# Sixteen dense matmuls ahead of the first scores of each full-attention loop

## The chip, the core and the metric

The program runs on one NeuronCore of one Trainium2 chip. The metric is the device time of one execution in microseconds (us), from the first to the last instruction. The profile's names for the engines are used: PE (TensorE, matmuls), PEld (its weight loads), DVE (VectorE), ACT (ScalarE), POOL (GpSimd).

## The reference, cut to what matters

Four residual blocks on x of shape (1, 2048, 512): local attention (A), full attention (B), A, B. Block B has 32 query heads of width 16 and one shared key/value head:

```python
def _B_ref(x, wq, wk, wv, wo):
    q = (x @ wq).reshape(B, S, H, Dh).transpose(0, 2, 1, 3)
    k = x @ wk
    v = x @ wv
    scores = einsum("bhqd,bkd->bhqk", q, k) * (Dh ** -0.5)
    p = softmax(scores, axis=-1)
    o = einsum("bhqk,bkd->bhqd", p, v)
    return o.transpose(0, 2, 1, 3).reshape(B, S, H * Dh) @ wo
```

## The kernel before

Block B is a prologue (layer norm, projections, and a flag that says whether exp may run without a maximum), then a loop over 2048 chunks of 128 keys x 512 queries of one head. Three chunks make a tile, so there are 683 tiles in a loop, and two loops.

```python
    def emit_scores(i):                       # PE: K = 32 rows per matmul, three of four row groups
        st = stp.tile([128, tile_chunks, 512], F32, name="st")
        for n, (qc, t, a, kt, g) in enumerate(cs):
            nc.tensor.matmul(st[:, n, :], lhsT=KAB[32 * g:32 * g + 32, a, ...],
                             rhs=QT[32 * g:32 * g + 32, t, ...], ..., tile_position=(32 * g, 0))

    def emit_exp(i):                          # ACT: one exp over 3 PSUM banks
        nc.scalar.activation(out=pt[...], in_=st_tiles[i][...], func=AF.Exp, scale=scale)

    def emit_outproj(n, now=None):            # PE: y, 128x128x512, four per block of 64 chunks
        ...
            y = ypp.tile([128, D], F32, name="y")
            nc.tensor.matmul(y[:], lhsT=onb[:, cols], rhs=wo_pad[:, t, a, :], start=True, stop=True)
            nc.vector.tensor_tensor(out=x_sb[:, qt, :], in0=x_sb[:, qt, :], in1=y[:], op=ALU.add)

    def emit_pv(i):                           # PE: all 128 rows, three of four groups of 32 columns
            nc.tensor.matmul(o_ps[(qc, t, a)][32 * g:32 * g + 32, :], lhsT=VE[:, kt, :],
                             rhs=pt[:, n, :], ..., tile_position=(0, 32 * g))

    for i in range(min(st_bufs, ntiles)):     # st_bufs = 2
        emit_scores(i)
    for i in range(ntiles):
        emit_exp(i)
        if i + st_bufs < ntiles:
            emit_scores(i + st_bufs)
        emit_pv(i)
        if i % op_every == op_every - 1:      # op_every = 3
            emit_outproj(1, now=i)
```

A scheduler then decides the order of the instructions on each engine; the program's order is only its starting point. PSUM, an on-chip memory, holds two st tiles of three chunks each, and one buffer each for o_ps and y.

## Time and profile before

| | before |
|---|---|
| device time, median of the first 3 runs | 2389.79 us (2388.62 to 2390.17) |
| attention loops, first exp to last exp | 955.2 and 956.3 us: 80% of the span |
| ACT busy in the loops | 97% |
| granted PE clock in the loops | 0.50 |
| an ordinary tile / a tile with a y | 1.34 us / 1.62 us |

From the page of the kernel before, the busy share in 40 equal slices of the span (9 is 90% or more), and the granted PE clock in tenths of full speed:

```profile
PE   5887899999999999999877879999999989999996
ACT  5314999999999999999842169999999999999996
PEclk9998555555555555555589975555555555555555
```

The clock is full for most of the local-attention blocks and half in both loops. In numbers, from the windows view (stretch in us, its length, then busy us and instruction count of PE, PEld, DVE, ACT and POOL, then clock, DMA share, GB/s). The first two lines are the two clock windows around the start of the first loop, the others lie inside the loops:

```profile
224.84:228.25 3.41, 1.02 (x4) 0.28 (x3) 2.33 (x5) 0.00 (x0) 0.00 (x0) 1.00 0.00 0
228.25:231.66 3.41, 1.06 (x6) 0.23 (x7) 0.33 (x3) 0.67 (x1) 0.38 (x1) 0.50 0.00 0
500.00:700.00 200.00, 181.94 (x886) 43.52 (x883) 57.48 (x63) 194.59 (x144) 0.00 (x0) 0.50 0.00 1
1600.00:1800.00 200.00, 182.10 (x886) 43.57 (x886) 53.27 (x60) 194.59 (x143) 0.00 (x0) 0.50 0.01 3
```

PE waits for the flag just before the loop, and the clock falls there. Inside, ACT is 97% busy and PE 91%.

The groups of instructions that carry the loop (count, then busy us and mean ns of one, then the engine's idle time before them and what ended most of it):

```profile
L511 ACT ACTIVATE pt<-st 128x1536 bf16<-128x1536 f32 (+1 forms) x1366 | 1860.7, 1508 | 63.9 <-PE st L503 62.0
L503 PE MATMUL st<-QT,KAB 32*128 32x512 bf16 x4096 | 859.4, 597 | 176.1 <-ACT pt L511 168.2
L520 PE MATMUL y<-wo_pad,onb 128*128 128x512 bf16 x256 | 155.3, 607 | 20.6 <-DVE onb L537 12.3
```

And the timeline of a stretch in which ordinary tiles turn into tiles with a y (start, duration, what, count, and in brackets the idle time just before and what ended it; lines of PEld and DVE are left out):

```profile
265.47 0.61 PE L503 MATMUL st<-QT,KAB 32*128 32x512 bf16 x3
...
266.81 0.61 PE L503 MATMUL st<-QT,KAB 32*128 32x512 bf16 x3 [0.18 <-ACT pt L511]
267.35 0.61 PE L547 MATMUL o_ps<-pt,VE 128*32 128x512 bf16 x3
267.90 0.61 PE L520 MATMUL y<-wo_pad,onb 128*128 128x512 bf16 x1
268.44 0.61 PE L503 MATMUL st<-QT,KAB 32*128 32x512 bf16 x3
...
269.52 0.61 PE L520 MATMUL y<-wo_pad,onb 128*128 128x512 bf16 x1
270.06 0.61 PE L503 MATMUL st<-QT,KAB 32*128 32x512 bf16 x3
...
272.41 1.45 ACT L511 ACTIVATE pt<-st 128x1536 bf16<-128x1536 f32 x1 [0.18 <-PE st L503]
```

Read the distance between the starts of two st groups. From 265.47 to 266.81 it is 1.34 us, and PE waits 0.18 us for ACT: ACT sets the pace. From 266.81 to 268.44, with a y, it is 1.63 us, without a wait on PE: PE sets the pace, and at 272.41 ACT waits for PE. Notice too that the y stand in consecutive tiles although the program emits one every three tiles. That is the scheduler's doing.

### The profile page before, as it was taken

How to read it: one execution, taken by the hardware profiler on the slowest of the kernel's cores; microseconds unless marked ns; L12 is line 12 of the kernel's file. 1: busy time of each engine (PE TensorE's matmuls, PEld its weight loads, DVE VectorE, ACT ScalarE, POOL GpSimd, SP SyncE). 2: the span in 40 equal slices, each digit the busy share in tenths (PEclk: the TensorE clock that was granted, in tenths of full speed). 3: DMA queues.
4: the chain of work that ended last, by engine and by line, in shares of the span. 5: the costliest groups of instructions: out<-in, count | busy, mean ns of one | idle time of the engine just before them, and what ended most of it. 6: DMA issues, size and time to landing. Idle time of an engine off the chain costs nothing.

```text
span 2389.7 us, 27720 instructions
## 1 busy us (share of the span) xinstructions
PE 2085.2 (87%) x11652; PEld 611.5 (26%) x11652; DVE 839.2 (35%) x1061; ACT 2015.7 (84%) x1603; POOL 35.7 (1%) x67
## 2 busy tenths in 40 slices
PE   5887899999999999999877879999999989999996
PEld 5433222222222222222153332222222222222221
DVE  3875222232223222322339832222222222222222
ACT  5314999999999999999842169999999999999996
POOL 1002000000000000000010000000000000000000
PEclk9998555555555555555589975555555555555555
DMA  1101000000000000000000000000000000000000
GB/s 63 37 2 28 1 1 1 1 1 1 1 1 1 1 1 1 1 1 1 1 3 2 1 1 1 1 1 9 1 1 1 1 10 1 1 9 1 1 1 11
DMA packets 14315, 11.56 MB, mean 5 GB/s; under 512 B 7904, under 2 KB 13536, under 8 KB 14048
## 3 DMA queue, kind: packets, MB, share of 16 engines
q1 hardware_dynamic: 13120, 8.60, 1.4%
q8 instruction: 95, 1.56, 0.3%
q10 hardware_dynamic: 1056, 1.05, 0.1%
q14 instruction: 44, 0.36, 0.1%
HBM read 7.37 MB, written 2.10 MB: 4 GB/s over the span
## 4 chain that ended last, share of the span: by engine, by line
ACT 39%; PE 31%; issue 17%; DVE 12%; POOL 0%; DMA 0%; ACTq 0%; SPq 0%; DVEq 0%; POOLq 0%
ACT pt L511 38%; PE st L503 11%; PE o_ps L547 8%; PE y L520 6%; DVE lb L536 3%; PE ps L184 3%; DVE prod L209 2%; PE y L265 1%; PE ps L359 1%; DVE pv L253 1%; PE acc L256 1%; DVE ot L528 1%; DVE lb L535 1%; DVE onb L537 1%; DVE qsq L373 0%
## 5 line engine op out<-in xcount | busy, mean ns | idle before, releaser
L511 ACT ACTIVATE pt<-st 128x1536 bf16<-128x1536 f32 (+1 forms) x1366 | 1860.7, 1508 | 63.9 <-PE st L503 62.0
L503 PE MATMUL st<-QT,KAB 32*128 32x512 bf16 x4096 | 859.4, 597 | 176.1 <-ACT pt L511 168.2
L547 PE MATMUL o_ps<-pt,VE 128*32 128x512 bf16 x4096 | 864.7, 607 | 1.4 <-ACT pt L511 1.0
L528 DVE COPY ot<-o_ps 128x512 f32<-128x512 f32 x64 | 44.3, 692 | 1163.2 <-PE o_ps L547 1163.2
L503 PEld LDWEIGHTS <-KAB 32*128 32x128 bf16 x4096 | 236.5, 99 | 766.1 <-issue 764.0
L547 PEld LDWEIGHTS <-VE 128*32 128x32 bf16 x4096 | 154.4, 101 | 621.4 <-issue 621.3
L521 DVE TENSOR_TENSOR x_sb<-x_sb,y 128x512 f32<-128x512 f32 x256 | 176.1, 688 | 226.1 <-PE y L520 226.1
L536 DVE RECIPROCAL lb<-lb 128x512 f32<-128x512 f32 (+1 forms) x70 | 214.9, 3075 | 2.1
L520 PE MATMUL y<-wo_pad,onb 128*128 128x512 bf16 x256 | 155.3, 607 | 20.6 <-DVE onb L537 12.3
L89 ACT ACTIVATE xn<-x_sb,ln_nmr,ln_rstd 128x512 bf16<-128x512 f32 x44 | 33.3, 806 | 92.0 <-DVE ln_nmr L83 88.8
L209 DVE TENSOR_TENSOR prod<-Qch,Kch 128x4096 bf16<-128x4096 bf16 x32 | 72.4, 2279 | 58.1 <-ACT Kch L188 56.7
L184 PE MATMUL ps<-xnT,w_sb 128*32 128x512 bf16 x1536 | 90.7, 392 | 1.9 <-ACT Vch L188 1.9
L184 PEld LDWEIGHTS <-w_sb 128*32 128x32 bf16 x1536 | 80.1, 141 | 12.1 <-issue 7.5
L256 PE MATMUL acc<-pv,ident 128*128 128x512 bf16 x256 | 68.7, 402 | 15.9 <-DVE pv L253 10.3
L212 PE MATMUL lg<-prod,ident 128*128 128x512 bf16 x256 | 60.6, 379 | 18.8 <-DVE prod L209 18.8
L258 ACT CAST Och<-acc 128x2048 bf16<-128x2048 f32 x8 | 14.9, 1866 | 72.2 <-PE acc L256 72.2
L253 DVE TENSOR_TENSOR pv<-attn,Vch 128x2048 bf16<-128x2048 bf16 x64 | 73.2, 1222 | 1.5 <-PE acc L256 1.5
L214 ACT ACTIVATE L<-lg 128x512 f32<-128x512 f32 x16 | 9.6, 598 | 70.7 <-PE lg L212 70.7
L99 PE MATMUL pT<-ident,xn 128*128 128x128 bf16 x256 | 27.6, 256 | 44.6 <-ACT xn L89 29.8
L520 PEld LDWEIGHTS <-onb 128*128 128x128 bf16 x256 | 26.4, 103 | 131.6 <-issue 89.7
L535 DVE STREAM_SHUFFLE lb<-ot 128x512 f32<-128x512 f32 (+1 forms) x70 | 46.8, 673 | 0.0
L537 DVE TENSOR_TENSOR onb<-ot,lb 128x512 bf16<-128x512 f32 (+1 forms) x70 | 44.6, 641 | 2.1
(89 smaller groups left out, 538.8 us busy)
## 6 DMA issues: line engine op xcount, KB each, us to landing
xi<-in_A_x_dram SPq DMA_DIRECT2D x4, 512.0 KB, 5.6
wo_r_73<-in_A_wo_dram SPq DMA_DIRECT2D x4, 512.0 KB, 8.2
w_sb<-in_A_wqkv_dram SPq DMA_DIRECT2D x4, 384.0 KB, 8.2
out_dram<-xo SPq DMA_DIRECT2D x2, 512.0 KB, 3.0
out_dram<-xo ACTq DMA_DIRECT2D x2, 512.0 KB, 4.9
wq_sb<-in_B_wq_dram SPq DMA_DIRECT2D x4, 128.0 KB, 3.2
woB_sb<-in_B_wo_dram SPq DMA_DIRECT2D x4, 128.0 KB, 3.7
wo_pad<-in_B_wo_dram SPq DMA_DIRECT2D x16, 32.0 KB, 1.8
```

Source lines behind the costliest of these rows:

```text
L184: nc.tensor.matmul(ps[32 * c:32 * c + 32, :], lhsT=wqkvP[:, kt, j, d, :], rhs=xnT[:, kt, c * 512:(c + 1) * 512], start=(kt == 0), stop=(kt ...
L209: nc.vector.tensor_tensor(out=prod[:], in0=Q[:, dsl, :], in1=K[:, dsl, PAD - DIL * w:PAD - DIL * w + 512], op=ALU.mult)
L253: nc.vector.tensor_tensor(out=pv[:], in0=attn[:, w, :].unsqueeze(1).to_broadcast([PCH, DG, 512]), in1=V[:, ds_, PAD - DIL * w:PAD - DIL * ...
L256: nc.tensor.matmul(acc[:, i, :], lhsT=ident[:PCH, :PCH], rhs=pv[:, i, :], start=(w == 0), stop=(w == W - 1))
L503: nc.tensor.matmul(st[:, n, :], lhsT=KAB[32 * g:32 * g + 32, a, kt * 128:(kt + 1) * 128], rhs=QT[32 * g:32 * g + 32, t, qc * 512:(qc + 1) ...
L511: nc.scalar.activation(out=pt[:, :len(cs), :], in_=st_tiles[i][:, :len(cs), :], func=AF.Exp, scale=scale)
L520: nc.tensor.matmul(y[:], lhsT=onb[:, cols], rhs=wo_pad[:, t, a, :], start=True, stop=True)
L521: nc.vector.tensor_tensor(out=x_sb[:, qt, :], in0=x_sb[:, qt, :], in1=y[:], op=ALU.add)
L535: nc.vector.stream_shuffle(out=lb[:, sl], in_=ot[:, sl], mask=[16] * 32)
L536: nc.vector.reciprocal(out=lb[:, sl], in_=lb[:, sl])
L537: nc.vector.tensor_tensor(out=onb[:, sl], in0=ot[:, sl], in1=lb[:, sl], op=ALU.mult)
L547: nc.tensor.matmul(o_ps[(qc, t, a)][32 * g:32 * g + 32, :], lhsT=VE[:, kt, :], rhs=pt[:, n, :], start=(kt == 0), stop=(kt == NT - 1), tile ...
```

## The change

The intent: PE is at half clock for the whole loop. A burst of dense matmuls raises the clock, so put one ahead of the first scores, so that the loop starts at full clock.

```diff
@@ attn_B_fast
+    warm = ypp.tile([128, D], F32, name="y")
+    pe_filler(nc, warm[:], wo_pad[:, 0, 0, 0:128], wo_pad[:, 0, 0, :], 16)
     for i in range(min(st_bufs, ntiles)):
         emit_scores(i)
```

`pe_filler` issues 16 matmuls of 128x128x512 into a tile that nobody reads. In PE's instruction order they stand after the branch on the flag and before the first scores; nothing else moves on any engine.

## The prediction

> **What bounds the kernel now.** The windows view gives each attention loop about 960 us (230-1190 and 1414-2375 us): 80% of the span. There ACT is 97% busy, PE 91%, granted clock 0.50 throughout. The timeline shows the two regimes. An ordinary tile takes 1.342 us and is set by ACT (eleven exps fill 14.88 us with no idle; PE waits 0.18 us per tile for ACT). A tile that also carries an output projection (y) takes 1.62 us and is set by PE: st, o_ps and y start 0.54 us apart. The groups list puts the whole price of the half clock at 62 us: ACT's idle time before the exps released by st. That, 2.6%, is the ceiling of what a full clock could give here.
>
> **What the change adds.** Sixteen 128x128x512 matmuls after the flag branch and before the first scores, twice, with nothing to overlap: the first exp needs the scores, which stand behind them on PE. Nothing is removed or reordered (I compared the instruction order). The existing filler at the end of the local-attention layer is the same shape: 16 per 3.41 us at full clock, 213 ns each; such dense matmuls took 427 ns at half clock. At half clock the burst lasts 6.8 us, at full 3.4.
>
> **The clock.** The Trainium skill, "TensorE: Matmul & The Clock Gate", Part 1, says the array is throttled by default, is released after a busy window of about 3.4 us and throttled again after an idle one. This trace's clock records agree on the length (every state lasts a multiple of 3.413 us) but not that only an idle window throttles. I counted streamed columns per window:
> - Released: windows with an array share near 1 (dense matmuls, four-way tiled matmuls), lowest 0.8.
> - Never released in 960 us: attention at half clock, 0.64 to 0.79 of the window streaming but only 3 of 4 row or column groups filled.
> - Throttled from full: windows streaming 0.25, 0.32, 0.33, 0.38 and 0.44. Kept for long: 0.5 and more.
>
> Just before each loop the clock falls (228 and 1412 us), since PE idles while the flag is computed. So the burst starts cold, runs cold for 3.4 to 6.8 us depending on where it meets the window grid, and finishes at full clock: 5.1 to 6.8 us, about 5.9. Then attention at full clock would stream 2 x 0.213 us per 1.342 us tile: 0.32 of a window, three quarters of the array. That is in the range that got throttled, so I expect the clock back at 0.50 within one or two windows (3.4-7 us), and it doesn't come back. In those windows no y exists, ACT sets the pace, so the full clock saves only about 0.3 us on the first scores.
>
> **Sum.** 2 x (5.9 - 0.3) = +11 us on the critical path, all of it: 2401 us, +0.5%. Range 2396 to 2405. Faster by over 2%: 0.05; within 2%: 0.93; slower: 0.02.
>
> **Right or wrong in the profile.** (1) A new group of 32 filler matmuls, about 12 us in all, with ACT idle about 12 us longer before the exps. (2) Clock 1.00 for one or two 3.41 us windows around the burst's end, then 0.50 for the rest of the loop. (3) Ordinary tiles still 1.342 us, y tiles 1.62 us, idle before exps by st otherwise about 62 us.
>
> **What would make it wrong.** If the loop holds the full clock once it has it (the throttle criterion could count time occupied, not columns), y tiles fall to ACT's 1.35 us and up to 62 us return: about 2340 us, just at the 2% line. If it holds for part of the loop, the result lies between. If the grid favours the burst, +9 us; if it never releases, +13.

## The result

The changed kernel took 2401.27 us (median of 4, 2392.05 to 2403.36) beside 2389.98 us of the kernel before: ratio 1.0045, interval 1.0023 to 1.0068. It is slower by about 11 us, clear of noise.

The clock row of the page of the changed kernel, and its groups:

```profile
PEclk9999555555555555555579985555555555555555
L511 ACT ACTIVATE pt<-st 128x1536 bf16<-128x1536 f32 (+1 forms) x1366 | 1860.5, 1513 | 75.3 <-PE st L503 73.2
L503 PE MATMUL st<-QT,KAB 32*128 32x512 bf16 x4096 | 857.4, 596 | 207.3 <-ACT pt L511 189.3
```

And the burst, from the list of groups that keeps shapes apart (30 of its 32 matmuls were recorded):

```profile
L111 PE MATMUL y<-wo_pad 128*128 128x512 bf16 x30 | 10.9, 527 | 5.4 <-DVE flags L399 5.1 <-issue 0.2
```

ACT's busy time is the same. Its idle time before the exps rose from 63.9 to 75.3 us, by 11.4 us, and the burst was busy for 10.9 us: these are the 11 us. The timeline of the first loop's head shows it happen. In the kernel before (PEld and other lines left out, here and below):

```profile
230.15 1.06 PE L503 MATMUL st<-QT,KAB 32*128 32x512 bf16 x6 [2.77 <-DVE flags L399]
230.99 14.88 ACT L511 ACTIVATE pt<-st 128x1536 bf16<-128x1536 f32 x11 [6.62 <-PE st L503]
```

and in the changed kernel:

```profile
229.79 4.43 PE L111 MATMUL y<-wo_pad 128*128 128x512 bf16 x10 [2.71 <-DVE flags L399]
234.44 1.56 PE L111 MATMUL y<-wo_pad 128*128 128x512 bf16 x5 [0.22 <-issue]
235.93 0.60 PE L503 MATMUL st<-QT,KAB 32*128 32x512 bf16 x6
236.53 26.97 ACT L511 ACTIVATE pt<-st 128x1536 bf16<-128x1536 f32 x20 [12.45 <-PE st L503]
...
239.37 0.39 PE L503 MATMUL st<-QT,KAB 32*128 32x512 bf16 x3 [0.62 <-ACT pt L511]
...
243.40 0.61 PE L503 MATMUL st<-QT,KAB 32*128 32x512 bf16 x3 [0.19 <-ACT pt L511]
```

The scores start at 235.93, 6.14 us after the burst does, and ACT waits 12.45 us for them instead of 6.62. At 239.37 a group of scores takes 0.39 us instead of 0.61, but PE only waits longer for ACT (0.62 instead of 0.18 us); ACT goes on without a gap. At 243.40 everything is as before. The clock windows around it, from the windows view cut at the clock's own steps, and a stretch of the loop:

```profile
228.25:231.66 3.41, 1.87 (x5) 0.74 (x6) 0.28 (x2) 0.00 (x0) 0.27 (x1) 0.50 0.03 5
231.66:235.08 3.42, 3.20 (x8) 1.22 (x8) 0.00 (x0) 0.00 (x0) 0.00 (x0) 0.50 0.00 0
235.08:238.49 3.41, 1.92 (x16) 0.50 (x14) 0.00 (x0) 1.96 (x2) 0.00 (x0) 1.00 0.00 0
238.49:241.90 3.41, 1.70 (x15) 0.66 (x13) 0.00 (x0) 3.41 (x4) 0.00 (x0) 1.00 0.00 0
241.90:245.32 3.42, 2.89 (x18) 0.75 (x17) 0.00 (x0) 3.42 (x4) 0.00 (x0) 0.50 0.00 0
500.00:700.00 200.00, 178.28 (x879) 43.45 (x883) 57.52 (x63) 194.50 (x144) 0.00 (x0) 0.50 0.00 1
```

Full clock for two windows, 235.1 to 241.9 us, then half for the rest of the loop.

Where the time lies, worked out from each trace as the first exp's start to the last exp's end of each loop, and the stretches around them (us). All experiments are in it, so that it need not be repeated:

```
kernel                     span   up to loop 1  loop 1  between  loop 2   tail
before                   2389.7       231.0      955.2    228.6    956.3   18.6
the change               2399.4       236.5      955.5    233.7    956.2   17.5
e1 burst of 32           2407.2       239.1      955.3    239.0    956.2   17.4
e2 burst on 32 rows      2401.2       236.7      955.3    235.4    956.3   17.5
e10 burst on 32 columns  2401.8       236.9      955.3    235.7    956.4   17.5
e7 burst in prologue     2385.0       228.0      955.5    227.7    956.2   17.7
e8 the change again      2389.7       231.8      955.2    229.0    956.2   17.5
e3 two per tile          2346.9       235.9      927.0    236.6    929.0   18.4
e5 one per tile          2333.7       233.0      922.4    234.0    926.8   17.5
e6 two, 32 columns       2344.9       233.6      927.6    236.3    929.9   17.4
e9 two, 32 rows          3298.4       233.6     1408.0    231.0   1407.0   18.8
e4 y spread out          2334.8       226.8      930.9    228.3    931.3   17.5
e11 e4 + e5 + e7         2327.1       228.0      932.0    227.4    922.6   17.2
e12 e4 + e5              2341.0       227.6      932.2    230.3    933.6   17.3
```

The change left both loops at 955 and 956 us. It lengthened the stretch before each by 5 us. 683 tiles at 1.331 us, the distance of exps that follow each other without a wait, would take 909 us, so each loop holds 46 us more than that. Counted from the starts of the exps, 17 us of it stand around the 32 copies of o_ps that end the blocks, and 29 us elsewhere, nearly all in tiles with a y.

### The profile page after: what moved, and what is told of

It reads as the page before. It is cut to its first block, busy times and chain, and to the rows that moved or that the text cites. A ratio compares the mean times of both kernels' runs of the same rounds, so it can differ in the third digit from the quotient of the medians. Undisturbed runs are those within 1.5% of the kernel's fastest.

```text
span 2399.4 us, 27700 instructions
## 1 busy us (share of the span) xinstructions
PE 2061.3 (86%) x11602; PEld 614.8 (26%) x11684; DVE 839.1 (35%) x1061; ACT 2015.3 (84%) x1603; POOL 35.6 (1%) x67
## 4 chain that ended last, share of the span: by engine, by line
ACT 37%; PE 33%; issue 17%; DVE 12%; POOL 1%; DMA 0%; SPq 0%; ACTq 0%; DVEq 0%; POOLq 0%
ACT pt L511 36%; PE st L503 11%; PE o_ps L547 10%; PE y L520 4%; DVE lb L536 3%; PE ps L184 3%; DVE prod L209 2%; PE y L265 1%; PE ps L359 1%; DVE pv L253 1%; PE acc L256 1%; DVE lb L535 1%; DVE ot L528 1%; DVE onb L537 1%; DVE ln_stats L79 0%
## 5 line engine op out<-in xcount | busy, mean ns | idle before, releaser
L511 ACT ACTIVATE pt<-st 128x1536 bf16<-128x1536 f32 (+1 forms) x1366 | 1860.5, 1513 | 75.3 <-PE st L503 73.2
L520 PE MATMUL y<-wo_pad,onb 128*128 128x512 bf16 x198 | 120.1, 606 | 16.4 <-DVE x_sb L521 15.8
```

The source lines that it names most:

```text
L511: nc.scalar.activation(out=pt[:, :len(cs), :], in_=st_tiles[i][:, :len(cs), :], func=AF.Exp, scale=scale)
```

## The experiments

The theory from the prediction: the burst costs its own duration, because ACT has nothing to do until the scores come; it does raise the clock, but attention at full clock uses too little of PE to keep it. The rivals: the burst is too small; the burst does harm in itself; the clock is worth nothing to this loop; what costs time in the loop is not the clock but the order. Further runs asked what it is about the work that raises and keeps the clock.

### e1: 32 instead of 16

```diff
-    pe_filler(nc, warm[:], wo_pad[:, 0, 0, 0:128], wo_pad[:, 0, 0, :], 16)
+    pe_filler(nc, warm[:], wo_pad[:, 0, 0, 0:128], wo_pad[:, 0, 0, :], 32)
```

> Theory (the burst pays only for itself; attention at full clock streams about 0.32 of a window and is throttled again): 16 more matmuls per loop run at full clock, 0.213 us each, so 3.4 us more per loop than with 16: about 2408 us (2404 to 2412). The clock stays at 1.00 during the longer burst and falls back to 0.50 at most two windows (6.9 us) after its end. Rival (a bigger run-up holds the clock for the loop): the clock stays at 1.00 long into the loop and the time falls below that of the kernel before, by up to 50 us.

Measured: 2405.54 us (ratio to before 1.0068, interval 1.0046 to 1.0091). The bursts lasted 9.45 and 9.77 us. The clock stood at 1.00 from 234.1 to 244.3 us, three windows of which the burst itself filled the first, and then at 0.50. A longer run-up buys nothing: the rival is out.

### e2 and e10: a burst on a quarter of the array, by rows and by columns

```diff
-    pe_filler(nc, warm[:], wo_pad[:, 0, 0, 0:128], wo_pad[:, 0, 0, :], 16)
+    for _ in range(16):                      # e2: 32 rows, 128 columns
+        nc.tensor.matmul(warm[:], lhsT=wo_pad[0:32, 0, 0, 0:128], rhs=wo_pad[0:32, 0, 0, :],
+                         start=True, stop=True, tile_position=(0, 0))
+    for _ in range(16):                      # e10 instead: 128 rows, 32 columns
+        nc.tensor.matmul(warm[0:32, :], lhsT=wo_pad[:, 0, 0, 0:32], rhs=wo_pad[:, 0, 0, :],
+                         start=True, stop=True, tile_position=(0, 0))
```

> Sixteen matmuls of the same length but on 32 of the 128 rows: the same streaming time, a quarter of the array. Theory (the throttle weighs how much of the array is filled): the clock is never released, the burst takes 16 x 0.427 = 6.8 us per loop, no window of the loop shows 1.00, time about 2404 us. Rival (the throttle counts only the time in which the array streams): released as with the dense burst, two windows at 1.00, about 2401 us.

> The head burst on 128 rows and 32 columns: a quarter of the array again, like the burst on 32 rows that didn't release the clock, but with all rows in use. If release weighs the filled share of the array: not released, no window of the loop at 1.00, about 2403 us. If it weighs the rows in use: released as with the dense burst, two windows at 1.00.

Measured: e2 2402.43 us (ratio 1.0058, interval 1.0035 to 1.0081), e10 2403.52 us (one run). The windows of e2, from the burst's second window on:

```profile
230.60:234.00 3.40, 3.40 (x9) 1.17 (x8) 0.00 (x0) 0.00 (x0) 0.00 (x0) 0.50 0.02 5
234.00:237.40 3.40, 2.94 (x11) 0.73 (x10) 0.00 (x0) 0.67 (x1) 0.00 (x0) 0.50 0.00 0
```

and of e10:

```profile
231.90:235.30 3.40, 3.40 (x9) 1.17 (x8) 0.00 (x0) 0.00 (x0) 0.00 (x0) 0.50 0.00 0
235.30:238.70 3.40, 1.91 (x17) 0.52 (x15) 0.00 (x0) 1.84 (x2) 0.00 (x0) 1.00 0.00 0
```

The two full windows (230.60 and 231.90) look alike: PE busy all the time, one matmul after another every 0.427 us, a quarter of the array filled. On 32 rows the clock stays at half, on 128 rows it rises. Both loops of each run agree. So neither the time in which PE is busy nor the share of the array decides; the rows in use do, or something that goes with them, such as the rows of data that are read: no run here tells these apart. The e2 burst lasted 16 x 0.427 = 6.8 us, of which 0.85 us ran beside scores on the other row groups.

### e7: the burst where PE idles anyway

The prologue has a switch for such a filler. Nothing is added at the loop's head.

```diff
-def layer_B(..., flag_slot=None, fillB=0,
+def layer_B(..., flag_slot=None, fillB=16,
```

> No burst at the loop's head; 16 dense matmuls in the prologue instead, in PE's idle time while the flag is computed (8 before the last n2 matmuls, where PE idles 1.9 us, 8 behind them, where it idles 2.7 us; 8 take 1.7 us at full clock). Theory: the burst's cost is its place on the path to the first scores, so here it costs nothing (within 1 us per loop); the loop starts at 1.00 and falls to 0.50 within two windows (up to 7 us), loops of 955.5 us as before; time within 2 us of the kernel before, 2387 to 2391 us. Rival (the dense burst itself slows the loop, for instance by a clock limit): about 2401 us again.

Measured: 2387.89 us over 6 runs (ratio 0.9998, interval 0.9983 to 1.0013), loops 955.5 and 956.2 us. The same sixteen matmuls cost nothing here. What the change costs is its place. They also gained nothing: in this run the clock fell at 229.5 us, 1.5 us after the first exp of the loop, and no y comes that early.

### e3 and e5: dense matmuls in every tile, to keep the clock

If the clock falls because attention at full clock uses PE too little, more work must keep it. The extra matmuls write into the st tile and are overwritten by the scores behind them.

```diff
         st_tiles[i] = st
+        for f in range(2):                   # e5: range(1)
+            nc.tensor.matmul(st[:, f, :], lhsT=wo_pad[:, 0, 0, 0:128], rhs=wo_pad[:, 0, 0, :],
+                             start=True, stop=True)
```

The head burst of the change stays in.

> The head burst as in the change, and two dense matmuls before the scores of every tile to hold the clock. At full clock the array share would be 0.24 + 2 x 0.213/1.342 = 0.56 of a window, streaming 0.64: windows like that kept the clock in the kernel before. Theory: the clock stays at 1.00 through both loops; y tiles fall from 1.62 us to ACT's 1.34 us; ACT's idle before the exps falls from 62 us to about 25; time about 2345 us (2335 to 2360). Caution: the scheduler also spreads the y matmuls over three tiles each in this build, so part of the gain may be the order. Rival 1 (attention can't hold the clock whatever is added): 0.50 and PE-bound tiles of about 2 us, so 2800 us or more. Rival 2 (the half clock costs nothing, ACT sets the pace everywhere): clock 1.00 but no gain, about 2401 us.

> The head burst as in the change and one dense matmul before the scores of every tile. In this build the four y of a block still stand in four tiles running, as in the kernel before, so a gain here is the clock's alone. At full clock the array share would be 0.24 + 0.213/1.342 = 0.40 of a window, streaming 0.48; the kernel before dropped a window of 0.44 and kept windows of 0.50, so it is open whether the clock holds. If it holds: a y tile needs about 1.3 us of PE, less than ACT's 1.34, so each loop takes about 930 us instead of 955.5 and the time is about 2350 us (2340 to 2360). If it doesn't: 3 x 0.54 = 1.6 us of PE per tile at half clock, 683 x 0.28 = 190 us more per loop, about 2750 us. If the gain of the two-matmul version was only the order of the y: clock 1.00, loops of 955 us, 2401 us.

Measured: e3 2342.6 us (ratio 0.9805, interval 0.9787 to 0.9823), e5 2338.42 us (0.9799, 0.9780 to 0.9818), a little below its range. The window of 0.44 that e5's expectation speaks of is a misreading, for which see the end. The clock held, in e3 from 233.8 to 1165.7 us. The stretch from 500 to 700 us, first of e3, then of e5:

```profile
500.00:700.00 200.00, 190.01 (x1211) 58.10 (x1211) 55.61 (x60) 198.78 (x149) 0.00 (x0) 1.00 0.00 1
```

```profile
500.00:700.00 200.00, 161.07 (x1063) 44.63 (x1066) 55.52 (x62) 199.28 (x149) 0.00 (x0) 1.00 0.00 1
```

ACT is above 99% busy, at clock 1.00. In e5 the y still stand in consecutive tiles, as before, so its gain is the clock's alone. From its timeline:

```profile
270.61 0.39 PE L523 MATMUL y<-wo_pad,onb 128*128 128x512 bf16 x1
271.00 0.38 PE L503 MATMUL st<-wo_pad 128*128 128x512 bf16 x1
271.30 0.39 PE L506 MATMUL st<-QT,KAB 32*128 32x512 bf16 x3
...
271.95 0.39 PE L523 MATMUL y<-wo_pad,onb 128*128 128x512 bf16 x1
```

A tile with a y now takes 271.95 - 270.61 = 1.34 us, ACT's pace, although it carries one more matmul. So the clock is worth 956 - 925 = 31 us per loop (loops of 922.4 and 926.8 us), 62 us in all, and the rival that it is worth nothing is out. In e5 the margin is thin: the clock fell once, at 1879 us, and came back 13.7 us later.

### e4: the order of the y, without any filler

In e3, but not in e5, the scheduler had spread the y out by itself. That called for a run of the order alone, at half clock and without a burst:

```diff
-            nc.tensor.matmul(y[:], lhsT=onb[:, cols], rhs=wo_pad[:, t, a, :], start=True, stop=True)
+            last_y[0] = nc.tensor.matmul(y[:], lhsT=onb[:, cols], rhs=wo_pad[:, t, a, :], ...)
+            order_after(tc, last_y[0], last_pv[0])     # behind the o_ps matmul emitted last
```

> No burst and no filler: the kernel before with each y matmul tied behind the o_ps of the tile at which the program emits it, so that the four y of a block stand three tiles apart in PE's order instead of in four tiles running. Rival to 'the half clock costs 62 us': the bunching costs it. An ordinary tile leaves PE 0.26 us free (1.342 less 2 x 0.54), and three tiles with one y need 3 x 1.08 + 0.54 = 3.78 us of PE against 3 x 1.342 = 4.03 us of ACT, so ACT should hardly wait: if the bunching is the cause, about 45 to 60 us less, 2330 to 2345 us, with the clock still 0.50. If the half clock itself is the cause, no change.

Measured: 2338.46 us (ratio 0.9793, interval 0.9771 to 0.9815), loops 930.9 and 931.3 us. From its timeline:

```profile
269.04 0.61 PE L522 MATMUL y<-wo_pad,onb 128*128 128x512 bf16 x1
269.58 0.61 PE L505 MATMUL st<-QT,KAB 32*128 32x512 bf16 x3
...
270.67 0.61 PE L505 MATMUL st<-QT,KAB 32*128 32x512 bf16 x3
...
271.98 0.61 PE L505 MATMUL st<-QT,KAB 32*128 32x512 bf16 x3 [0.16 <-ACT pt L513]
...
273.07 0.61 PE L522 MATMUL y<-wo_pad,onb 128*128 128x512 bf16 x1
```

After each y PE catches up: the next two tiles take 1.09 and 1.31 us, and at 271.98 PE waits for ACT again before the next y. The group of exps in this kernel shows what is left:

```profile
L513 ACT ACTIVATE pt<-st 128x1536 bf16<-128x1536 f32 (+1 forms) x1366 | 1839.2, 1588 | 36.0 <-PE st L505 35.8
```

Most of what the full clock can give, 25 of 31 us per loop, is to be had at half clock by order alone. The clock was at 0.50 throughout the loops. Counted as above, the first loop of e4 keeps 18 us around the copies of o_ps and 4 us elsewhere, that of e5 12 us and 1 us. So order and clock both remove the stall of the y; what the clock removes besides is a part of the wait at the changes of block.

### e6 and e9: keeping the clock with narrow matmuls

Two per tile as in e3, but on a quarter of the array: e6 on 128 rows and 32 columns, e9 on 32 rows and 128 columns. e9 uses the row group of the first score, in that score's bank.

```diff
         st_tiles[i] = st
+        for f in range(2):                   # e6
+            nc.tensor.matmul(st[0:32, f, :], lhsT=wo_pad[:, 0, 0, 0:32], rhs=wo_pad[:, 0, 0, :],
+                             start=True, stop=True, tile_position=(0, 0))
+        for f in range(2):                   # e9 instead
+            gq = cs[0][4]
+            nc.tensor.matmul(st[:, 0, :], lhsT=wo_pad[32 * gq:32 * gq + 32, 0, 0, 0:128],
+                             rhs=wo_pad[32 * gq:32 * gq + 32, 0, 0, :], start=True, stop=True,
+                             tile_position=(32 * gq, 0))
```

> As the kernel with the head burst and two matmuls per tile, but the two use 32 of the 128 columns of the array: the same streaming time (0.64 of a window at full clock), array share only 0.24 + 0.08 = 0.32. If staying at full clock depends on the filled share of the array: throttled within two or three windows of the burst, PE-bound tiles of 4 x 0.5 = 2 us, 2 x 683 x 0.6 = 800 us more, about 3200 us. If it depends on the time in which the array streams: 1.00 through both loops and about 2345 us.

> As the run with two narrow matmuls per tile, but narrow in rows (32 of 128) instead of columns (32 of 128). That run kept the clock at an array share of 0.32, so the filled share of the array is not what keeps it; it may be the rows in use or the streaming time. At full clock: streaming about 0.63 of a window in both; share of rows in use 0.60 there, 0.36 here. If streaming time keeps the clock: 1.00 through both loops, about 2345 us. If the rows in use do: throttled within three windows, PE-bound tiles of about 1.8 us, 2950 us or more.

Measured, one run each: e6 2346.85 us, e9 3300.33 us. The stretch from 500 to 700 us, e6 and then e9:

```profile
500.00:700.00 200.00, 188.39 (x1197) 47.86 (x1203) 54.03 (x61) 198.76 (x148) 0.00 (x0) 1.00 0.00 1
```

```profile
500.00:700.00 200.00, 198.11 (x793) 39.08 (x794) 40.86 (x48) 140.18 (x98) 0.00 (x0) 0.50 0.00 1
```

With all rows in use the clock holds, although only a third of the array is filled on average. With 32 rows it fell within two windows and never came back in the loop, and PE then paced the loop at 2.06 us per tile (1408/683), more than the 1.8 us expected. It is the rows again: the windows before the two falls streamed for 0.48 and 0.60 of their time with a row use of 0.37 and 0.34, those of e6 inside its loops, streaming for 0.52 to 0.76, had a row use of 0.47 and more.

### What the clock follows, over all traces

For every clock window of 3.413 us in the fourteen traces I worked out three shares from the matmul records (start, shape, columns streamed at the granted clock): the time in which any matmul streams, the same weighted with the part of the array filled, and the same weighted with the rows in use out of 128 (matmuls on different row groups at the same time add up). The windows before a trace's first clock record count as half clock: the matmuls there start 0.427 us apart. Then I looked for the one threshold per share that best tells the windows after which the clock changed:

```
                          4159 windows at full clock       some 5800 at half clock   
                          121 of them followed by half     121 of them followed by full
weighted by               best threshold, misplaced        best threshold, misplaced
rows in use               0.355,   7                       0.745,   4
array filled              0.205,  52                       0.745,   8
time streaming only       0.36,   13                       0.895,  38
```

Rows do best on both sides; most windows are clear-cut by any of the three, so it is the pairs e2/e10 and e6/e9 that carry the argument. With rows, the overlap at full clock lies between 0.36 and 0.39. Some matmul records are missing from traces, which makes a share too low, and this settles three of the four misplaced at half clock (0.63 to 0.66 before a rise in the loops of e5, e11 and e12). Each of these windows lacks one y matmul, whose weight load and whose add on DVE are recorded. With it they reach 0.75 to 0.78. When all missing y of the loops are put back in all traces in this way, rows misplace one window at half clock, the filled array 8 and the time 38. The one left (e8 at 1209.3 us, 0.69, transposes only) lacks no record that I can see and stays open. So, on this core: below a row use of about 0.37 in a window the full clock falls, and from about 0.75 the half clock rises. This describes the traces that it was fitted on; it is not a statement of how the hardware is built.

It explains the loop. At full clock an ordinary tile streams its scores for about 0.216 us on three row groups and its o_ps for 0.216 us on all rows: (0.75 + 1) x 0.216 / 1.34 = 0.28 of the window, below 0.37, so it falls. One dense matmul more adds 0.16: 0.44, and holds, with little to spare. At half clock the busiest windows of the kernel before reach 0.74, just too little to rise by themselves.

### e8: the change again

> The change again, for the spread of its times: one of its four runs took 2392 us and the others 2401 to 2403. Theory: the burst costs 3.4 to 6.8 us per loop depending on where it meets the free-running windows, so runs between +6 and +13 us, 2395 to 2403, centre 2400; a run at 2392 should be rare and be as low as the lowest runs of the kernel before at that moment. Loops of 955.5 us in the profile, clock at 1.00 for two windows of each.

Measured: 2398.1 us (6 runs, 2391.45 to 2403.26), ratio 1.0043, interval 1.0025 to 1.0061. The profiled run was one of the two low ones, 2391.45 and 2391.8 us; so runs as low as this are not rare, which I had expected them to be. Its loops were 955.2 and 956.2 us and its bursts 5.50 and 5.73 us, 11.2 us in all, as before. It was short in the stretches before the loops (231.8 and 229.0 us against 236.5 and 233.7). Its clock record has fewer windows at half clock in the local-attention blocks: between 127 and 185 us it never falls, where the first profile of the change fell at 163 us, and before the third block's projections it rises at 1213 us, not at 1228. So the low runs are a matter of where the clock windows meet the rest of the program; the grid of the windows is not tied to it (the first clock record lies between 33.9 and 37.3 us in the fourteen traces). The other traces agree. Without prologue filler, PE's first instruction behind the flag of loop 1 starts at 225.7 to 226.7 us in the six traces whose clock holds for 58 us from about 127 us on (e4, e5, e6, e8, e9, e12), and at 228.9 to 230.3 us in the six whose clock also falls near 163 us. That accounts for the low profile; that it accounts for each single time is likely and not shown. The kernel before shows a similar spread (2382.01 to 2391.25 us in these rounds).

### e11 and e12: put together

e11 is e4's order, e5's one matmul per tile and e7's filler in the prologue, without the burst at the head. e12 is e11 without the prologue filler.

> What the runs point to, put together: the y three tiles apart, one dense matmul per tile to keep the clock, and the 16 dense matmuls in the prologue's idle time instead of at the loop's head. Loops of 920 to 927 us instead of 955.7, and no burst on the path: 2 x 32 us less than the kernel before, about 2325 us (2316 to 2334); clock 1.00 nearly all the way. If the clock adds nothing to the spread order, loops of 931 us and about 2338 us.

> The same without the 16 matmuls in the prologue: is any run-up needed? The loop starts at 0.50 with tiles bound by PE at about 1.6 us, streaming 0.80 of a window. If such windows release the clock (in the run with one matmul per tile it fell once in mid-loop and came back after 13.7 us), it comes within about 15 us, for a loss of some 3 us per loop: about 2331 us. If they don't, 2 x 683 x 0.27 us more: about 2700 us.

Measured over 5 runs each: e11 2334.94 us (ratio 0.9777, interval 0.9754 to 0.9801), just above its range, e12 2344.47 us (0.9811, 0.9797 to 0.9826). The second loop of e11 ran at full clock from its start and took 922.6 us, as expected. In its first loop the clock fell at 229.2 us and rose only at 280.4, so that loop took 932.0. In e12 the clock rose 54 and 59 us after the start of the loops, not within 15 us as I had expected: at half clock those windows use 0.73 to 0.74 of the rows, a hair below the threshold. What carried them over it was a y. The first y of a loop comes some 51 us after its start, in e12 here (the matmul's own record is missing, but not its weight load and its add):

```profile
278.35 0.61 PE L553 MATMUL o_ps<-pt,VE 128*32 128x512 bf16 x3
278.89 0.10 PEld L525 LDWEIGHTS <-onb 128*128 128x128 bf16 x1 [0.44 <-issue]
279.30 0.63 PE L505 MATMUL st<-wo_pad 128*128 128x512 bf16 x1 [0.33 <-issue]
279.54 0.69 DVE L527 TENSOR_TENSOR x_sb<-x_sb,y 128x512 f32<-128x512 f32 x1 [8.99 <-PE st L508]
```

The clock rose at 281.3 us, at the end of that window; in e11 too at the end of the window with the first y, in e12's second loop of that with the second (row use 0.747, recorded in full). So a run-up is not needed, but it saves some 9 us where it works. e11 has the lowest ratio, 2.2% below the kernel before; against e4 alone (ratio 0.9793, in other rounds) the intervals overlap, as with e3 and e5, so that the clock adds to the order is shown for loop 2 of the trace, but not for the whole time.

## Why the prediction was right

- **The time.** 2401 us was predicted, 2401.27 measured; six more runs gave 2398.1. The range 2396 to 2405 held the medians. It did not hold every run: 2391 and 2392 occurred. That the first median came within 0.3 us is luck, as single runs spread over 12 us; what the runs support is some 10 us (ratios 1.0045 and 1.0043).
- **The burst is on the critical path.** Right. Its first matmul to the first score took 6.14 and 4.86 us, 11.0 in all, against 2 x 5.9 predicted. The second lies below the predicted 5.1 to 6.8: that burst ran cold for only 2.7 us, not 3.4 or more, because the window that it filled to 0.78 was enough. e1 (longer burst, longer time) and e7 (same matmuls in idle time, ratio 0.9998) show that the place is the cost.
- **The burst starts at half clock and ends at full clock.** Right: matmuls every 0.427 us, then every 0.216 us (the prediction and the expectations write 0.213).
- **The clock falls again within two windows and doesn't come back.** Right, 6.8 us after it rose, in both loops. e3 and e5 show the converse: more work keeps it.
- **The reason for it: columns streamed in three quarters of the array.** Right only in direction. Neither the streaming time nor the filled part of the array fits the runs; the rows in use do (e2 against e10, e6 against e9). The list that the step rests on is also off. By a recount of the trace before, the clock fell after windows that streamed for 0 to 0.39 of their time; the window of about 0.44 (at 183.9 us) kept it, and the next one, 0.25, lost it. In the loop the windows stream for 0.59 to 0.81, not 0.64 to 0.79.
- **First scores faster at full clock.** Right, 0.24 us per loop (from scores to exp 0.84 us before, 0.60 after).
- **"The whole price of the half clock at 62 us."** The number came out, by luck; the step behind it failed, without harm to the sum, as no clock was kept. Measured by loop length, the full clock is worth 31 us per loop or 62 us in all (e5). But the 62 us of the prediction are ACT's idle time before exps, which contain the waits at the two loop heads (6.6 and 6.4 us) and leave out that exps which stand back to back overlap and stalled ones don't (ACT's busy time for the same exps is 1860.7 us before and 1839.2 in e4). Nor is it the price of the half clock alone: 25 of the 31 us per loop are also had at half clock by order (e4). It is for the most part the same stall: order and clock together (second loop of e11, 922.6 us) give no more than the clock alone (e5, 922.4). A stall put down to a slow engine was for the most part a matter of when the work was asked of it.

## What to carry to other kernels

A run-up for the PE clock is worth having only if the work behind it keeps the clock: work out the row use of the steady loop at full clock first (here 0.28, and it took 0.44 to hold). Put any run-up where PE idles: between the branch and the first work of the loop it cost its whole length here. And before buying clock, look whether the tiles in which PE is the slowest stand in a row: spreading them over tiles with slack gained 2.1% here with no added work.

## What the Trainium skill lacked or had wrong

- "TensorE: Matmul & The Clock Gate", Part 1 and the table "Why this matters for your kernels": it says that the full clock is lost after an idle window, and advises against idle gaps of over about 3 us. (Its section on a second failure mode does tell of a clock that goes up and down when PE idles briefly and often, without a measure.) Here it was lost after windows without any such gap: in the changed kernel from 238.5 to 241.9 us PE never idled more than 0.62 us, with a row use of 0.25. Its 3.413 us window agrees: every complete clock state in the records is a multiple of it.
- The same page, Part 1: the clock is said to rise after a busy window. In the kernel before PE was 91% busy for 955 us at half clock and it didn't rise. What counts is missing from the page: the rows in use, with about 0.75 of a window to rise and 0.37 to stay (a fit over fourteen traces; matmuls on 128 rows and 32 columns raised the clock and held it, those on 32 rows and 128 columns did neither).
- The same page, Part 4: transposes are said not to raise the clock. In the kernel before the window at 1207.9 us holds nothing but transposes (`nc.tensor.transpose`, 27 recorded, row use 0.78), and the next window was granted 1.00. The trace doesn't mark the mode that the page means, so that these are of it is not shown.
- "TensorEngine Tiling (Array Packing)" doesn't say what tiling does to the clock. Matmuls in one of four row groups left PE at half clock in e2 (busy for all of a 3.40 us window) and lost the full clock in e9; those in one of four column groups raised it in e10 and kept it in e6.
- "Trainium Kernel Development and Optimization", Performance Expectations, calls matmul busy time a bad measure of how close a kernel is to its limit (roofline). Nothing is wrong here, and these runs agree that it tells little: PE was 91% busy in the kernel before, at half clock, and 81% busy in e5 (161.07 of 200 us) at full clock with more work.
